# An mLSTM, gMLP and channel-mix kernel: the block mask's load moved forward, and two small copies given to GpSimd

## The chip, the cores and the metric

The kernel runs on one NeuronCore of a Trainium2 chip. The metric is the device time of one execution in microseconds. Engines are named as in the profile: PE is the matrix engine (PEld its weight loads), DVE the vector engine, ACT the scalar engine, POOL is GpSimd, SP is the engine that issues nearly all transfers. A q behind a name (SPq) means the engine's instruction queue.

## The reference

Three stages follow each other; the output of one is the input of the next. B is 2, H is 8 heads, S is 768 tokens, D is 40.

```python
# stage 1: a gated recurrence, token by token (m is the running maximum of the gates)
C = f_stab * C + i_stab * outer(v_t, k_t)          # per batch and head, 40 x 40
n = f_stab * n + i_stab * k_t
y_t = sigmoid(o_t) * (C @ q_t) / max(|n . q_t|, 1)
# stage 2, on x = y as (B, S, 320)
h = relu(x @ w_in); u, v = h[:512], h[512:]
x = (u * (w_spatial @ layernorm(v) + b_spatial)) @ w_out
# stage 3: channel mix with the token before
xk, xr = mu * x + (1 - mu) * x_prev                 # two sets of mu
out = sigmoid(xr @ w_r) * (relu(xk @ w_k) ** 2 @ w_v)
```

The output is float32, and so are the inputs, except `w_in`, `w_out`, `w_k`, `w_v` and `w_r`, which come in float64.

## The kernel before, in words

**Tiling.** The recurrence is computed in chunks of 128 tokens: 6 chunks for each of 2 batches, taken alternately, which makes 12 positions. At a position PE forms scores of queries and keys (`sc`, line 463), the logarithms of the decays (`ld`, lines 471 to 497), their product with the values (`av`, line 599), the chunk's contribution to the state (`sp`, line 533) and the state's contribution to the tokens (`ip`, line 570). ACT takes the exponential of `ld` into `dt` (lines 479 and 505), DVE multiplies `dt` by the scores (lines 489 and 508), and `normalise` (from line 602) makes the chunk's output `x`. PE transposes `x` through `tp` (line 646); ACT and DVE split the transposed tile into two float32r parts, `xg` (lines 660 and 235). Stage 2's first product (`up`, `vp`) is then drawn between the positions. Stages 2 and 3 follow as long rows of float32r products with three terms each (line 671).

**The mask.** A product of eight heads in groups of three puts blocks that belong to different heads side by side. The block mask, three columns of 120 rows, cuts them out. It is loaded into `bm_raw` with a stride of 41 elements (so each element stands alone in memory), copied by ACT to `bm_sb` (line 546), and used by ACT at the first chunk of each batch (`cn`, line 548) and by DVE later (line 552).

**The 64 repeated columns.** `x` has 384 columns, of which 320 come from the recurrence. The last 64 repeat columns 256 to 319 so that the third transpose fills both halves of its 128 rows. The copy (lines 627 and 628) is done by ACT at the first two positions and by POOL at the other ten.

**Weights.** A float64 weight is loaded as raw words and turned into a high and a low float32r part: ACT makes `wsq` (line 274), DVE or ACT the bits (`wbits`), DVE combines them (lines 284 and 288), ACT writes the high part (line 297), POOL the low part (line 235). For `w_u` there are three slices, split one after the other in the first 33 us; `wsq` has two buffers.

**What sets the order.** While the program is built, a planner keeps a clock of its own and an estimate for each step. Every chain of steps, such as `("P", 0.2, ...)`, names its engine (V is DVE, A is ACT, P is POOL) and a cost; the planner always issues the step that it expects to start first, and PE's tasks with it. The result is a fixed list for PE, ACT, DVE and POOL, which each work through in that order. Where the planner expects PE to wait, it inserts short matmuls with unused results (`wp`, line 363). SP issues transfers in the order of the calls, and a transfer waits until the eighth before it has landed.

**Lines to follow.** The loads at the start stand at lines 370 to 372: the two gates, the identity, four tiles of output gates (`og`), then the first queries and keys (`qk`). The next group, with `bm_raw` sixth among its eight, stands at lines 874 to 876. The gate tiles of the chunks from the third on are computed on DVE at lines 407 to 416 (`f`, `i`, in 96 rows), and PE transposes them at line 423 (`gpsc`).

Of the kernel before, what the change touches and what calls it, by code (L numbers as in the profile page):

```python
# [7 lines left out]
F32 = mybir.dt.float32  # L8
# [10 lines left out]
def tile_mlstm_gmlp_channelmix(  # L19
# [25 lines left out]
    SEQ = [6 * b + c for c in range(6) for b in range(2)]  # L45
    P = 128
    H, D = 8, 40
    DA = D + 1
# [3 lines left out]
    DM = H * D  # L52
# [6 lines left out]
    vec, act, pool, pe = nc.vector, nc.scalar, nc.gpsimd, nc.tensor  # L59
    sync = nc.sync  # L60
# [4 lines left out]
    at = tc.alloc_tile_pool(name="at", bufs=1, side="right")  # L65
# [59 lines left out]
    def use(e, cost, t=None):  # L125
        free[e] = max(free[e], clock[0] if t is None else t) + cost
        return free[e]
# [45 lines left out]
    def chain(key, *steps, ready=None):  # L173
        running.append(Chain(key, steps, clock[0] + 0.2 if ready is None else ready, 0.0))

    def finish(*keys, stall=True):
        for k in keys:
            while any(b[0] == k or b[0][0] == k for b in back):
                if not force_feed():
                    break  # L180
            for c in [c for c in running if c.has(k)]:
                while c in running and c.has(k):
                    advance(c.start(), skip=c)
                    if not c.open():
                        finish(split[0], stall=False)
                    if c in running and c.has(k):
                        issue(c)
        if stall:
            at_least(max([done.get(k, 0.0) for k in keys], default=0.0))
# [25 lines left out]
    def load(out, in_, kb, after=0.0):  # L215
        sync.dma_start(out=out, in_=in_)  # L216
        dma_free[0] = max(dma_free[0], after, clock[0] - 1.0) + max(0.5, kb / (360.0 if clock[0] > 20.0 else 230.0))
        return dma_free[0] + 1.8

    def page(name, dt=F32R, n=PG, keys=()):  # L220
        own("pg", 12, *keys)
        return base.tile([P, n if dt == I64 else PG], dt, tag="pg", name=name, bufs=12)[:, :n]
# [80 lines left out]
    def rows3(t, w):  # L303
        return t[:, :3 * w].rearrange("p (a b) -> p a b", a=3)
# [6 lines left out]
    fg = gp.tile([16, S], F32, name="fg")  # L311
    ig = gp.tile([16, S], F32, name="ig")
# [17 lines left out]
    def load_qk(i):  # L330
        b, c = divmod(i, NCH)
        t = at.tile([P, 2, 4, P], F32, tag="qk", name=f"qk{i}", bufs=2)
        for hh in range(2):
            e = load(t[64 * hh:64 * hh + D], qk[b, c, hh], 164)
        st["q", i], st["k", i] = t[:, 0], t[:, 1]
        st["at", i] = e

    def load_kv(i):
        b, c = divmod(i, NCH)
        n = H * D + H * DA + (3 * P if c > 0 else 0)  # L340
        t = at.tile([P, H * D + H * DA + 3 * P], F32, tag="kvq", name=f"kvq{i}", bufs=2)
        note(("kv", i), load(t[:, :n], kvq[b, c, :, :n], n * 0.5))
        st["kt", i] = t[:, :H * D].rearrange("p (h d) -> p h d", h=H)
        st["vt", i] = t[:, H * D:H * (D + DA)].rearrange("p (h d) -> p h d", h=H)
        if c > 0:
            st["qc", i] = t[:120, H * (D + DA):].rearrange("p (g t) -> p g t", g=3)

    def load_o(c):
        for b in range(B):
            o = st["o", b, c] = at.tile([P, DM], F32, tag="og", name=f"og{c}_{b}", bufs=9)  # L350
            st["ot"] = load(o, o_tok[b, c // 3, :, c % 3], 164)
# [15 lines left out]
    vec.memset(unit.bitcast(F32), 0.0)  # L367
    for t in first_.values():
        vec.memset(t.bitcast(F32), 0.0)
    for a in 'f i d o0 o1 q'.split():  # L370
        dict(f=lambda: sync.dma_start(out=fg, in_=f_gate), i=lambda: sync.dma_start(out=ig, in_=i_gate),
             d=lambda: sync.dma_start(out=id_sb, in_=ident), o=lambda: load_o(int(a[1])), q=lambda: load_qk(SEQ[0]))[a[0]]()

    pool.memset(ones, 1.0)
# [227 lines left out]
    def normalise(i):  # L602
        b, c = divmod(i, NCH)
        av, spare = st.pop(("av", i)), st.pop(("spare", i))
        osl = st["o", b, c].rearrange("p (h d) -> p h d", h=H)
        nn = st.pop(("nn", i)) if c > 0 else at.tile([P, H, DA], F32, tag="nn", name=f"nn{i}", bufs=2)
        dn = at.tile([P, H], F32, tag="dn", name=f"dn{i}", bufs=2)
        x = at.tile([P, 3 * P], F32, tag="x", name=f"x{i}", bufs=2)

        finish(*[("nn", i)] * (c > 0), stall=False)  # L610

        def clip():
            vec.tensor_scalar(out=spare, in0=nn[:, :, D], scalar1=1.0, scalar2=None, op0=ALU.max)
            pool.tensor_tensor(out=osl, in0=osl, in1=nn[:, :, :D], op=ALU.mult)
            return use("P", 0.82, free["V"])

        chain(("x", i),
              ("V", 0.41, lambda: vec.tensor_tensor(out=nn, in0=nn, in1=av, op=ALU.add)) if c > 0 else
              ("A", 0.4, lambda: act.copy(nn, av)),
              ("V", 0.08, clip),  # L620
              ("V", 0.15, lambda: vec.scalar_tensor_tensor(out=dn, in0=nn[:, :, D], in1=spare,
                                                           scalar=-1.0, op0=ALU.mult, op1=ALU.max), ("av", i)),
              ("V", 0.18, lambda: vec.reciprocal(out=dn, in_=dn)),
              ("V", 0.4, lambda: vec.tensor_tensor(out=x[:, :DM].rearrange("p (h d) -> p h d", h=H), in0=osl,
                                                   op=ALU.mult,
                                                   in1=dn.unsqueeze(2).to_broadcast([P, H, D]))),
              ("P", 0.2, lambda: pool.tensor_copy(x[:, DM:], x[:, 2 * P:DM])) if SEQ.index(i) >= 2 else
              ("A", 0.2, lambda: act.copy(x[:, DM:], x[:, 2 * P:DM])))
        st["x", i] = x

    xg = {}
# [139 lines left out]
    def w_in_load(nm, j, *qs):  # L771
        W.setdefault((nm, "raw"), [])
        for q in qs:
            raw = page(f"w_in{nm}{q}", I64, PG // 2, [f"w_{nm}{x}" for x in range(3)])[:, :512]
            W[nm, "raw"].append((q, raw, load(raw, w_in[j, q], 512)))
# [84 lines left out]
    free["A"] = 8.5  # L860
    free["P"] = 3.0
    hu = [rows3(page(f"w_u{q}"), 512) for q in range(2)]
    bm_raw = at.tile([120, 3], F32, name="bm_raw")
    m2 = gp.tile([96, 2, P], F32, name="m2")
    lpk = gp.tile([96, 6 * NCH], F32, name="lpk")
    clock[0] = 5.5
# [4 lines left out]
        for w in range(2):  # L871
            st["late"] = load(m2[:, w], mg[:, w:w + S], 48, 14.0)

    for a in 'k0 v0 q6 k6 v1 b v2 n'.split():
        dict(k=lambda: load_kv(SEQ[a != "k0"]), q=lambda: load_qk(SEQ[1]), n=lambda: load_qk(SEQ[2]),
             v=lambda: w_in_load("u", 0, int(a[1])), b=lambda: load(bm_raw, blockmask[:, 0:3 * DA:DA], 2))[a[0]]()
    w_in_split("u", hu)
# [42 lines left out]
    def position(p):  # L920
# [45 lines left out]
        def n1():  # L966
            intra(i, 1)
            normalise(i)
            if nn is not None:
                load_kv(nn)  # L970
            if p == 0:
                w_in_load("v", 1, 0)
                sync.dma_start(out=mu_sb, in_=mu)
            if p == 1:
                w_in_load("v", 1, 1)
                load_o(2)
                load_o(3)
            if p == 2:
                w_in_load("v", 1, 2)
                load_o(4)  # L980
            if p == 3:
                load_o(5)
            if n is not None:
                key_weights(n)
# [225 lines left out]
    for g in range(2 * B):  # L1210
# [17 lines left out]
        for j in range(3):  # L1228
            sl = slice(j * P, (j + 1) * P)
            prs = []  # L1230
            for f in range(8):
                k0, k1 = k2t[g, f][:, 0, sl], k2t[g, f][:, 1, sl]
# [126 lines left out]
```

## Time and profile before

| | us |
|---|---|
| median of 3 runs | 308.97 |
| lowest, highest | 307.27, 309.54 |
| the profiled execution's own time | 308.54 |
| its span, first to last instruction | 305.5 |

| engine | busy us | share of the span |
|---|---|---|
| PE | 294.4 | 96% |
| DVE | 218.5 | 72% |
| ACT | 172.4 | 56% |
| POOL | 140.3 | 46% |

Times in the rows count from the start of the span. A row of the timeline gives the start, the duration, the engine, the line, the operation, out<-in, the shapes and the count; a bracket at its end is the idle time of the engine just before it, and what ended that. Engines overlap neighbouring instructions a little, so a row can start some 0.1 us before the one ahead of it ends. [...]

### The profile page before, as it was taken

The numbers are of one execution on the slowest core, as the hardware profiler recorded it, in microseconds if no ns is written. First come the engines' busy times: TensorE is split into PE (matmuls) and PEld (weight loads), VectorE is DVE, ScalarE is ACT, GpSimd is POOL, SyncE is SP. The second block draws the span as 40 slices with busy tenths as digits, with TensorE's granted clock in tenths as the row PEclk, the third lists the DMA queues.
The fourth block names the chain that finished last, engine by engine and source line by source line (L and its number), as shares of the span: only waits on it lengthen the run. The fifth ranks groups of instructions, "written<-read, shape, count | busy, mean of one in ns | idle before, by whom it ended". The sixth has DMA issues, their size and how long they took to land.

```text
span 305.5 us, 6000 instructions
## 1 busy us (share of the span) xinstructions
PE 294.4 (96%) x2233; PEld 273.3 (89%) x2233; DVE 218.5 (72%) x440; ACT 172.4 (56%) x383; POOL 140.3 (46%) x167
## 2 busy tenths in 40 slices
PE   8998898999889999999999999999999999999995
PEld 6776787787778887999999999999999999999995
DVE  7768696856697787746879989898856755745611
ACT  3764587676865555653254654686936845734610
POOL 5143324526679774733556637484426305303500
PEclk9999999999999999999999999999999999999999
DMA  6959665333223411554115212221010010000001
GB/s 154 291 165 288 195 226 171 137 116 114 56 69 98 138 46 50 174 157 165 43 45 172 81 41 86 89 86 44 3 43 21 2 43 24 0 35 32 1 21 43
DMA packets 13939, 28.77 MB, mean 94 GB/s; under 512 B 2407, under 2 KB 7783, under 8 KB 13911
## 3 DMA queue, kind: packets, MB, share of 16 engines
q1 hardware_dynamic: 13879, 28.33, 29.4%
q8 instruction: 17, 0.28, 0.4%
q0 software_dynamic: 32, 0.07, 0.2%
q14 instruction: 11, 0.09, 0.1%
HBM read 26.20 MB, written 1.97 MB: 92 GB/s over the span
## 4 chain that ended last, share of the span: by engine, by line
PE 71%; DVE 9%; ACT 6%; POOL 5%; DMA 4%; issue 2%; SPq 1%; POOLq 0%; DVEq 0%; ACTq 0%
PE spp L671 16%; PE kp L671 15%; PE vv L671 14%; PE wop L671 7%; PE up L671 5%; PE rp L671 5%; DMA bm_raw<-in_blockmask_dram 3%; PE vp L671 2%; DMA qk<-in_qk_dram 2%; POOL vn L235 2%; PE sc L463 1%; DVE sb L728 1%; DVE dt L508 1%; PE av L599 1%; SPq L216 1%
## 5 line engine op out<-in xcount | busy, mean ns | idle before, releaser
L1202 POOL TENSOR_TENSOR sq<-sq 128x384 f32<-128x384 f32 x32 | 29.9, 941 | 47.9 <-ACT sq L1201 47.8
L671 PE MATMUL spp<-wsp,vn 128*128 128x384 f32 x288 | 50.4, 334 | 0.0
L671 PEld LDWEIGHTS spp<-wsp,vn 128*128 128x128 f32 x288 | 49.9, 188 | 0.0
L671 PE MATMUL kp<-xk,wk 128*128 128x384 f32 x256 | 45.3, 334 | 0.0
L671 PEld LDWEIGHTS kp<-xk,wk 128*128 128x128 f32 x256 | 44.4, 188 | 0.0
L671 PE MATMUL vv<-wv,k 128*128 128x320 f32 x288 | 42.9, 309 | 0.0
L671 PEld LDWEIGHTS vv<-wv,k 128*128 128x128 f32 x288 | 42.4, 188 | 0.0
L235 DVE TENSOR_TENSOR k<-sq,k 128x384 fp32r<-128x384 f32 x32 | 26.2, 820 | 13.6 <-ACT k L1203 13.6
L671 PE MATMUL up<-xg,w_u 128*128 128x256 f32 x192 | 31.0, 295 | 0.0
L671 PE MATMUL vp<-w_v,xg 128*128 128x512 f32 x96 | 29.0, 417 | 1.9 <-ACT vr L740 0.9
L1099 POOL TENSOR_TENSOR vs<-vs,u 128x384 f32<-128x384 f32 x16 | 19.8, 1237 | 22.5 <-DVE vs L1098 21.1
L671 PEld LDWEIGHTS up<-xg,w_u 128*128 128x128 f32 x192 | 25.8, 190 | 1.0 <-DVE xg L235 0.2
L1201 ACT ACTIVATE sq<-kp 128x384 f32<-128x384 f32 x32 | 15.6, 490 | 16.8 <-PE kp L671 14.8
L284 DVE SCALAR_TENSOR_TENSOR wbits<-wsq,wbits 128x320 int32<-128x320 int32 (+1 forms) x27 | 20.9, 774 | 4.4 <-ACT wsq L274 3.5
L671 PE MATMUL wop<-gt,wo 128*128 128x384 f32 x128 | 22.8, 334 | 0.0
L671 PEld LDWEIGHTS wop<-gt,wo 128*128 128x128 f32 x128 | 22.2, 188 | 0.0
L671 PEld LDWEIGHTS vp<-w_v,xg 128*128 128x128 f32 x96 | 17.0, 189 | 5.7 <-ACT vr L740 1.4
L1242 DVE TENSOR_TENSOR ob<-rs,vv 128x320 f32<-128x320 f32 x12 | 5.8, 487 | 20.4 <-PE vv L671 19.3
L235 POOL TENSOR_TENSOR vn<-vr,vn 128x512 fp32r<-128x512 f32 x12 | 15.4, 1287 | 6.8 <-ACT vn L750 6.8
L1100 ACT CAST gt<-vs 128x384 fp32r<-128x384 f32 x16 | 8.2, 512 | 18.0 <-POOL vs L1099 18.0
L288 DVE SCALAR_TENSOR_TENSOR wsq<-wraw,wbits 128x320 int32<-128x320 int32 (+1 forms) x21 | 17.2, 821 | 0.3
L1141 DVE SCALAR_TENSOR_TENSOR tm<-x,mu_sb,tm 128x384 f32<-128x384 f32 x24 | 17.1, 748 | 0.0
(184 smaller groups left out, 571.4 us busy)
## 6 DMA issues: line engine op xcount, KB each, us to landing
kvq<-in_kvq_dram SPq DMA_DIRECT2D x10, 516.0 KB
qk<-in_qk_dram SPq DMA_DIRECT2D x24, 160.0 KB
wraw<-in_w_k_dram SPq DMA_DIRECT2D x6, 512.0 KB
wraw<-in_w_v_dram SPq DMA_DIRECT2D x8, 320.0 KB
wraw<-in_w_sp_dram SPq DMA_DIRECT2D x12, 192.0 KB
og<-in_o_tok_dram SPq DMA_DIRECT2D x12, 160.0 KB
out_dram<-ob SPq DMA_DIRECT2D x12, 160.0 KB
w_inu<-in_w_in_dram SPq DMA_DIRECT2D x3, 512.0 KB
```

The source lines that it names most:

```text
L216: sync.dma_start(out=out, in_=in_)
L235: eng.tensor_tensor(out=out, in0=a, in1=b.bitcast(F32), op=ALU.subtract)
L284: vec.scalar_tensor_tensor(out=t["bits"], in0=t["sq"].bitcast(I32), scalar=3, in1=t["bits"], op0=ALU.logical_shift_left, op1=ALU.bitwise_or)
L288: vec.scalar_tensor_tensor(out=t["sq"].bitcast(I32), in0=t["high"], scalar=SIGN, in1=t["bits"], op0=ALU.bitwise_and, op1=ALU.bitwise_or)
L463: pe.matmul(st["sc", i, x][:, h * P:(h + 1) * P], k_[64 * x:64 * x + D, h, :], q_[64 * x:64 * x + D, h, :], start=True, stop=True)
L671: pe.matmul(out[0], l, x, start=j == 0, stop=j == len(prs) - 1)
L1099: ("P", 1.29, lambda: pool.tensor_tensor(out=vs, in0=vs, in1=ut[b][:, d, sl], op=ALU.mult)),
L1100: ("A", 0.51, lambda: act.copy(gt[:, 0], vs)), ("V", 0.7, lambda: sub(vec, gt[:, 1], vs, gt[:, 0])))
L1141: return lambda: vec.scalar_tensor_tensor(out=t[:, c], in0=x[:, c, 1:], scalar=mu_sb[:, w, c:c + 1], in1=t[:, c], op0=ALU.mult, op1=ALU.add)
L1201: chain(("k2", g, f), ("A", 0.49, lambda: act.activation(out=sq, in_=ps, func=AF.Relu), ("kp", g, f)), ("P", 0.96, lambda: pool.tensor_ten ...
L1202: ("P", 0.96, lambda: pool.tensor_tensor(out=sq, in0=sq, in1=sq, op=ALU.mult)),
L1242: vec.tensor_tensor(out=ob, in0=rs, in1=ps, op=ALU.mult)
```

## The change

The load of `bm_raw` is issued fourth, right behind the identity, and no longer between the second and the third slice of `w_u`. The copy of the 64 columns goes to POOL at all twelve positions.

```diff
-    for a in 'f i d o0 o1 q'.split():
-        dict(f=lambda: sync.dma_start(out=fg, in_=f_gate), i=lambda: sync.dma_start(out=ig, in_=i_gate),
+    bm_raw = at.tile([120, 3], F32, name="bm_raw")
+    for a in 'f i d b o0 o1 q'.split():
+        dict(b=lambda: load(bm_raw, blockmask[:, 0:3 * DA:DA], 2), f=lambda: sync.dma_start(out=fg, in_=f_gate), i=lambda: sync.dma_start(out=ig, in_=i_gate),
...
-              ("P", 0.2, lambda: pool.tensor_copy(x[:, DM:], x[:, 2 * P:DM])) if SEQ.index(i) >= 2 else
-              ("A", 0.2, lambda: act.copy(x[:, DM:], x[:, 2 * P:DM])))
+              ("P", 0.2, lambda: pool.tensor_copy(x[:, DM:], x[:, 2 * P:DM])))
...
-    bm_raw = at.tile([120, 3], F32, name="bm_raw")
...
-    for a in 'k0 v0 q6 k6 v1 b v2 n'.split():
+    for a in 'k0 v0 q6 k6 v1 v2 n'.split():
```

The planner makes another order of the second edit. On SP only `bm_raw` moves. Three places where the lists differ:

ACT at the first transpose, before: the copy of the 64 columns, then the high part of the first slice of `w_u`, then the split of the transposed `x`.

```order
L278 ACTIVATE wbits<-w_inu_162 128x512
L628 COPY x_347<-x_347 128x64
L297 CAST w_u_148<-wsq 128x512
L660 CAST xg_412<-tp_413 128x3x128
L274 ACTIVATE wsq<-w_inu_165 128x512
```

And with the change:

```order
L278 ACTIVATE wbits<-w_inu_163 128x512
L660 CAST xg_407<-tp_408 128x3x128
L297 CAST w_u_150<-wsq 128x512
L274 ACTIVATE wsq<-w_inu_165 128x512
L278 ACTIVATE wbits<-w_inu_165 128x512
```

The copy has left ACT, and the split of `x` stands ahead of the first slice of `w_u`. On PE the transposes `tp` of that `x` stand behind ten of the short matmuls that follow `av`, where they stood behind twelve; two more stand behind them.

ACT some ten instructions later, before: the second copy and the high part of the third slice of `w_u` stand ahead of the exponential of the fourth position.

```order
L414 CAST Axc<-i_77 96x128
L628 COPY x_489<-x_489 128x64
L297 CAST w_u_148<-wsq 128x512
L479 ACTIVATE dt_0_539<-ld_0_532 128x512
L426 ACTIVATE egc<-gpsc 128x192
L910 ACTIVATE dec<-dps 120x36
```

And with the change:

```order
L415 CAST Axc<-i_77 96x128
L480 ACTIVATE dt_0_538<-ld_0_531 128x512
L427 ACTIVATE egc<-gpsc 128x192
L909 ACTIVATE dec<-dps 120x36
L297 CAST w_u_150<-wsq 128x512
```

The third slice stands behind the exponential `dt` and behind `egc` and `dec`, which it preceded.

DVE around the gate tiles `f` and `i`, before:

```order
L288 SCALAR_TENSOR_TENSOR wsq<-w_inu_162,wbits 128x512
L284 SCALAR_TENSOR_TENSOR wbits<-wsq,wbits 128x512
L407 TENSOR_TENSOR f_76<-f_76,m_151 96x128
L408 TENSOR_TENSOR i_77<-i_77,m_151 96x128
L409 TENSOR_TENSOR f_76<-f_76,m_151 96x128
```

And with the change:

```order
L288 SCALAR_TENSOR_TENSOR wsq<-w_inu_163,wbits 128x512
L408 TENSOR_TENSOR f_76<-f_76,m_152 96x128
L409 TENSOR_TENSOR i_77<-i_77,m_152 96x128
L410 TENSOR_TENSOR f_76<-f_76,m_152 96x128
L411 SCALAR_TENSOR_TENSOR f_76<-ones,f_76 96x128
```

The bits of the third slice (line 284) no longer stand between the second slice and the gate tiles; they stand behind the `x` of the second position, fifteen instructions later.

## Rows read from the trace of the kernel before

**Rows 1.** The chain that ended last, 8 to 33 us: start, us, what.

```profile
8.79 8.23 DMA bm_raw<-in_blockmask_dram
```

**Rows 2.** Windows: us, busy (count) of PE, PEld, DVE, ACT, POOL; clock, DMA, GB/s.

```profile
60.00:305.50 245.50, 239.34 (x1682) 228.65 (x1678) 172.22 (x320) 135.51 (x296) 116.45 (x128) 1.00 0.21 67
```

**Rows 3.** Timeline of PE, 14 to 37 us.

```profile
14.91 1.13 PE L463 MATMUL sc<-qk 40*128 40x128 f32 x14 [0.28 <-DMA qk<-in_qk_dram]
15.97 0.83 PE L533 MATMUL sp<-kvq,kw 128*120 128x123 f32 x6
...
18.80 2.02 PE L363 MATMUL wp<-id_sb 128*128 128x256 bf16 x12
20.66 0.49 PE L646 MATMUL tp<-id_sb,x 128*128 128x128 f32 x3
...
27.38 0.48 PE L471 MATMUL ld<-unit,Axb 128*128 128x512 f32 x1 [0.59 <-DVE dt L489]
...
29.50 0.30 PE L423 MATMUL gpsc<-id_sb,i 96*128 96x96 f32 x1 [0.71 <-DVE i L416]
...
32.27 0.80 PE L533 MATMUL sp<-kvq,kw 128*120 128x123 f32 x6 [1.22 <-ACT dt L479]
...
34.06 0.49 PE L646 MATMUL tp<-id_sb,x 128*128 128x128 f32 x3
...
36.04 0.86 PE L671 MATMUL up<-xg,w_u 128*128 128x256 f32 x5
```

**Rows 4.** Timeline of ACT, 17 to 32 us.

```profile
17.04 0.19 ACT L546 COPY bm_sb<-bm_raw 120x3 f32<-120x3 f32 x1 [1.84 <-DMA bm_raw<-in_blockmask_dram]
17.32 0.82 ACT L548 ACTIVATE cn<-sp,bm_sb 40x123 f32<-40x123 f32 x3
...
20.19 0.25 ACT L628 COPY x<-x 128x64 f32<-128x64 f32 x1
20.52 0.62 ACT L297 CAST w_u<-wsq 128x512 fp32r<-128x512 f32 x1
21.19 0.48 ACT L660 CAST xg<-tp 128x384 fp32r<-128x384 f32 x1
...
24.16 0.59 ACT L479 ACTIVATE dt<-ld 128x512 f32<-128x512 f32 x1
...
31.01 0.62 ACT L297 CAST w_u<-wsq 128x512 fp32r<-128x512 f32 x1 [0.36 <-DVE wsq L288]
31.54 0.59 ACT L479 ACTIVATE dt<-ld 128x512 f32<-128x512 f32 x1
```

**Rows 5.** Timeline of SP's queue.

```profile
2.18 1.85 SPq L216 DMA_DIRECT2D og<-in_o_tok_dram  x4
...
16.85 0.59 SPq L216 DMA_DIRECT2D m<-mg  x1
```

**Rows 6.** Waits of SP's queue, 16 to 17.6 us: us, times, longest.

```profile
SPq L216 <- DMA w_inu<-in_w_in_dram: 0.6, 1, 0.6
```

**Rows 7.** Timeline of POOL, 24 to 47 us.

```profile
24.33 1.27 POOL L235 TENSOR_TENSOR w_u<-wsq,w_u 128x512 fp32r<-128x512 f32 x1 [1.85 <-ACT w_u L297]
...
46.88 0.56 POOL L627 COPY x<-x 128x64 f32<-128x64 f32 x1 [1.59 <-PE up L671]
```

**Rows 8.** Timeline of DVE, 19 to 30 us.

```profile
19.80 0.68 DVE L288 SCALAR_TENSOR_TENSOR wsq<-w_inu,wbits 128x512 int32<-128x512 int32 x1
...
23.78 0.69 DVE L284 SCALAR_TENSOR_TENSOR wbits<-wsq,wbits 128x512 int32<-128x512 int32 x1 [0.62 <-ACT wbits L278]
24.39 1.36 DVE L407 TENSOR_TENSOR f<-f,m 96x128 f32<-96x128 f32 x1
...
25.88 0.28 DVE L409 TENSOR_TENSOR f<-f,m 96x128 f32<-96x128 f32 x1
...
26.64 0.69 DVE L489 TENSOR_TENSOR dt<-dt,sc 128x512 f32<-128x512 f32 x1
...
28.82 0.63 DVE L416 TENSOR_SCALAR i<-i,f 96x128 f32<-96x128 f32 x1
```

## The prediction

> **What bounds the kernel now.** I read three views in turn. First the chain of waits that ended last. The conspicuous piece that is not compute is the mask's load: issued at 8.79 us, landed 8.23 us later, at 17.02 [rows 1]. It invites the conclusion that 8 us can be had; the next views show why not. Second, the busy time by windows: from 60 us to the end PE works 239.34 of 245.50 us at the full granted clock [rows 2]. That stretch has little to give, and since it works through one fixed list, what the head of the program gains or loses reaches the end nearly one for one. Third, PE's timeline of the head. PE has no gap at 17 us, where ACT waits for the mask: it works through its list and through the short `wp` matmuls. What it does wait for stands in the brackets [rows 3]: 0.28 us at 14.91 for the second position's `qk`, 0.59 at 27.38 for a product on DVE, 0.71 at 29.50 for the gate tile `i` of DVE, 1.22 at 32.27 for the exponential `dt` of ACT. Only these four can be shortened or lengthened by the change; together they are 2.8 us of 305.5.
>
> **The mask's wait itself.** ACT stood idle for 1.84 us before `bm_sb` [rows 4]. But the next instruction, `cn` at 17.32, also needs PE's `sp`, which ran from 15.97 to 16.80 [rows 3]. An early mask therefore gives ACT at most 17.32 - 16.80 = 0.52 us, and the next paragraph takes most of it back. I put it at nothing: `cn` stays near 17.3, and with it `x` of the first position.
>
> **The load in its new place.** Four issues of `og` take 1.85 us of SP's queue, 0.46 each [rows 5]. One more in front of them sends everything up to the second position's `qk` a slot later. PE was already waiting for that `qk` at 14.91, so PE goes on at 15.37: a loss of 0.46 that its gapless list carries on. The other price is what the small elements cost the transfer engines. SP's `m` at 16.85 waited for a `w_inu` slice to land, the transfer ahead of the mask [rows 5, 6]; the mask landed at 17.02, 0.17 behind it. So the bounds are 0.17 (only the engines' time counts) and 0.63 (both). I take the slot, 0.46, because the first transfers leave SP one slot apart, which is more than the 0.17.
>
> [...]
>
> **The first copy on POOL.** ACT's copy took 0.25 us at 20.19 [rows 4]. POOL's has been seen to take 0.56 [rows 7]; `x` is done just after DVE's `wsq` starts at 19.80 [rows 8], so the copy ends near 20.45. The transposes now stand behind ten `wp` and not twelve. Twelve took 18.80 to 20.66, 0.155 each; ten, with PE 0.46 later, put the transposes at 20.66 - 0.31 + 0.46 = 20.81. The copy is covered by the `wp`; were they gone, PE would wait some 0.3 us for it.
>
> **The first slice of `w_u` gets later.** ACT's split `xg` follows the transposes by 0.53 (21.19 against 20.66), so 21.34. The cast of `w_u`, which was ahead of it at 20.52, now follows it: 21.34 + 0.48, less an overlap of 0.1, is 21.72, a delay of 1.20 us. Behind it hang POOL's low part, the `wsq` buffer that this frees, the third slice's bits, the second slice and the exponential `dt` at 24.16 [rows 4], now 25.36 to 25.95.
>
> **DVE still comes out ahead.** Before, DVE did the bits of the third slice at 23.78, then `f` at 24.39, which took 1.36 us where the same form takes 0.28 at 25.88; the product `dt` followed at 26.64 [rows 8]. During `f` POOL ran its `w_u` part from 24.33 to 25.60 [rows 7], and `f` ended 0.15 us after it. Now the bits are out of the way. DVE's second `wsq` may be held by POOL's first part (21.72 + 0.62 + 0.08 + 1.27 = 23.7), takes 0.68, then `f`, `i`, `f` at 0.28 and a scan of 0.42 end near 25.6. The product then waits for the exponential only: 26.0, 0.64 earlier. PE's wait at 27.38 goes: PE arrives there at 26.79 + 0.46 = 27.25 and finds the bank free.
>
> [...]
>
> **The gate tile `i`.** From the product at 26.64 to the end of `i` at 28.82 + 0.63 = 29.45 DVE needed 2.81 us [rows 8]. From 26.0 that ends at 28.81. But POOL's second `w_u` part, 1.2 us later than at 24.33, now falls into these instructions. One hold as long as that of `f`, 1.36 - 0.28 = 1.08, would make it 29.89. Between the two I take the middle, 29.35. PE's second `gpsc` starts 0.05 later, at 29.40.
>
> **The wait of 1.22 us.** PE's `sp` at 32.27 would have started at 31.05 without it, 1.55 behind `gpsc`. The exponential it waited for ran at 31.54, late because the cast of the third `w_u` slice stood ahead of it at 31.01 and itself waited for DVE [rows 4]. In the new order it comes before that cast; its `ld` starts at 27.25 and it can run before 29. So `sp` starts at 29.40 + 1.55 = 30.95, not 32.27: **a gain of 1.32 us**. With `i` at 28.81 or 29.89 it is 1.86 or 0.78; with the load's bounds the ends are 2.15 and 0.61.
>
> **What is late next.** The third slice: bits and combination follow `x` of the second position (29.35 + 0.4 + 0.5 = 30.3), 0.69 and 0.68, so 31.6; cast 32.2; POOL's part of 1.27 until 33.5. Its first reader is the run of `up` at 36.04 [rows 3], 34.7 by then: 1.2 us to spare. The second copy on POOL follows `x` at 30.3; if both DVE steps hold it off, it is done by 31.9, and its transposes, at 34.06 before, come at 32.74. Both are covered; without cover each would cost what it is late. Nothing further on changes its order.
>
> **The sum.** 308.54 - 1.3 = 307.2 for the execution that was profiled, whose span is 305.5 and which has 3.0 us around it. The median of the runs is 0.43 higher; from it the sum gives 307.7. I predict between them, **307.4**.
>
> **Rivals.**
> [...]
> - *More goes than I count.* If the earlier load costs only 0.17 and DVE is not held at all, the gain is 2.15; if waits further on, which I leave unchanged, shrink as well (PE is idle 6.2 us after 60 us), 3 to 4. This gives 304.9 to 306.5. For it: POOL and DVE meet at other moments throughout. Against: most of that list is unchanged.
> - *Slower: the mask holds up the first loads.* The transfer took 8.23 us, and how much of it was its own 360 elements is not separable in these rows beyond the 0.17 above. If at the head they delay `qk` by a third of that, 2.7 us, the time is 308.97 - 1.3 - 0.46 + 2.7 = 309.9. It decides from a delay of 0.46 + 1.32 = 1.8 us. Against: the slot and the 0.17.
> - *The load's move does nothing* is part of the forecast: `sp` covers its wait.
>
> **Chances.** Forecast 0.56 (306.5 to 308.1), waits back 0.19, more 0.19, slower 0.06. The range leaves out the far half of "more" and the slower case: 305.6 to 309.2. A measurement of this kernel can tell 1%, 3.1 us, from no change. Below 305.9 lies half of "more" and a sliver of the forecast: 0.13. Above 312.0 lies half of the slower case: 0.04 with what I have not thought of. The rest, 0.83, is within 1%.
>
> **What would show it.** `bm_sb` runs near 15.3 without a wait; PE's `sc` waits some 0.5 us longer for `qk`; `f` on DVE starts before 24.4 and takes less than 1.36; PE's `sp` (the one at 32.27) waits for nothing and starts near 31; the transposes at 34.06 come near 32.7. A wait at `sp` or `gpsc` as long as before, or `sc` later than 16.0, would make the prediction wrong, as would a shift at 36 us that has gone or doubled by the end.

## The result, and the profile after

| | before | changed |
|---|---|---|
| median, us | 308.85 (20 runs) | 305.31 (20 runs) |
| lowest, highest | 306.63, 312.05 | 304.53, 312.68 |
| ratio, 95% interval | | 0.9895 [0.9873, 0.9918] |

The change gains 3.5 us, about 1%. The ratio is taken over fast executions, within 1.5% of the fastest of their kernel (19 and 17 of the 20). 307.4 was predicted, and 305.6 to 309.2 as the range: the waits that the prediction named do go, but the change is worth more than they are long. The first profiled execution of the changed kernel was interrupted by one late transfer (further down), so the rows of after come from its repetition, whose span is 303.2 us and whose mean granted clock is 0.998.

PE's timeline of that execution, to be held against [rows 3]: start, duration, engine, line, operation, out<-in, shapes, count, and in brackets the idle time just before it and what ended that.

```profile
9.46 0.39 PE L476 MATMUL ld<-mask 128*128 128x512 bf16 x1 [1.68 <-ACT mask L859]
...
15.09 1.24 PE L464 MATMUL sc<-qk 40*128 40x128 f32 x16
...
27.02 0.48 PE L472 MATMUL ld<-unit,Axb 128*128 128x512 f32 x1
...
28.59 0.30 PE L424 MATMUL gpsc<-id_sb,i 96*128 96x96 f32 x1 [0.15 <-DVE i L417]
...
29.98 0.73 PE L534 MATMUL sp<-kvq,kw 128*120 128x123 f32 x6
...
31.70 0.49 PE L646 MATMUL tp<-id_sb,x 128*128 128x128 f32 x3
...
33.67 0.86 PE L671 MATMUL up<-xg,w_u 128*128 128x256 f32 x5
```

The waits of 0.59 us at `ld` and 1.22 us at `sp` are gone, and 0.15 of the 0.71 us at `gpsc` is left. `sp` starts 2.29 us earlier (29.98 against 32.27), the transposes 2.36, `up` 2.37, and the span is 2.3 shorter than the 305.5 of before: what the head gains reaches the end whole. A wait that the first trace did not have stands at 9.46; it is explained with the load, below.

ACT's timeline, to be held against [rows 4]:

```profile
16.05 0.18 ACT L547 COPY bm_sb<-bm_raw 120x3 f32<-120x3 f32 x1
17.21 0.82 ACT L549 ACTIVATE cn<-sp,bm_sb 40x123 f32<-40x123 f32 x3 [0.98 <-PE sp L534]
...
21.16 0.48 ACT L660 CAST xg<-tp 128x384 fp32r<-128x384 f32 x1 [0.66 <-PE tp L646]
21.54 0.62 ACT L297 CAST w_u<-wsq 128x512 fp32r<-128x512 f32 x1
...
28.17 0.60 ACT L480 ACTIVATE dt<-ld 128x512 f32<-128x512 f32 x1 [1.04 <-PE ld L476]
...
30.82 0.62 ACT L297 CAST w_u<-wsq 128x512 fp32r<-128x512 f32 x1 [1.37 <-DVE wsq L288]
```

The mask is there before ACT wants it, and `cn` then waits for PE's `sp`, at 17.21 against 17.32. The exponential `dt` runs at 28.17, not 31.54, and the third slice's cast waits for DVE behind it, where it delays nobody.

DVE, against [rows 8], and then POOL, against [rows 7]:

```profile
22.43 1.62 DVE L288 SCALAR_TENSOR_TENSOR wsq<-w_inu,wbits 128x512 int32<-128x512 int32 x1
23.98 0.28 DVE L408 TENSOR_TENSOR f<-f,m 96x128 f32<-96x128 f32 x1
...
25.82 0.69 DVE L490 TENSOR_TENSOR dt<-dt,sc 128x512 f32<-128x512 f32 x1 [0.71 <-ACT dt L480]
26.43 0.37 DVE L413 TENSOR_TENSOR i<-i,f 96x128 f32<-96x128 f32 x1
...
27.91 0.63 DVE L417 TENSOR_SCALAR i<-i,f 96x128 f32<-96x128 f32 x1
```

```profile
19.83 0.63 POOL L628 COPY x<-x 128x64 f32<-128x64 f32 x1 [0.59 <-DVE x L625]
22.24 1.27 POOL L235 TENSOR_TENSOR w_u<-wsq,w_u 128x512 fp32r<-128x512 f32 x1 [1.77 <-ACT w_u L297]
25.37 1.28 POOL L235 TENSOR_TENSOR w_u<-wsq,w_u 128x512 fp32r<-128x512 f32 x1 [1.87 <-ACT w_u L297]
```

POOL's first part of `w_u` now lies beside DVE's `wsq`, which takes 1.62 us where it took 0.68 [rows 8], and DVE has the time for it. The second part, 25.37 to 26.65, lies beside the product `dt`, which takes its usual 0.69; the step of `i` that starts in its last 0.2 us takes 0.37, 0.09 more than the 0.28 of the other steps of this form.

### The profile page after: what moved, and what is told of

The parts are those of the page before. It is cut to its first block, busy times and chain, and to the rows that moved or that the text cites. A ratio compares the mean times of both kernels' runs of the same rounds, so it can differ in the third digit from the quotient of the medians.

```text
span 307.9 us, 5999 instructions
## 1 busy us (share of the span) xinstructions
PE 296.8 (96%) x2233; PEld 275.9 (90%) x2233; DVE 218.6 (71%) x440; ACT 172.5 (56%) x381; POOL 141.1 (46%) x169
## 4 chain that ended last, share of the span: by engine, by line
PE 77%; ACT 6%; DVE 6%; POOL 4%; DMA 2%; issue 2%; SPq 1%; POOLq 0%; ACTq 0%; DVEq 0%
PE spp L671 16%; PE kp L671 14%; PE vv L671 14%; PE wop L671 7%; PE up L671 6%; PE rp L671 5%; PE sc L464 3%; PE vp L671 2%; PE av L600 2%; PE sp L534 2%; POOL vn L235 2%; DMA og<-in_o_tok_dram 1%; DVE sb L728 1%; PE wp L363 1%; PE ip L571 1%
## 5 line engine op out<-in xcount | busy, mean ns | idle before, releaser
L671 PE MATMUL up<-xg,w_u 128*128 128x256 f32 x192 | 32.1, 304 | 0.0
L671 PEld LDWEIGHTS up<-xg,w_u 128*128 128x128 f32 x192 | 26.9, 198 | 0.9
```

The source lines that it names most:

```text
L671: pe.matmul(out[0], l, x, start=j == 0, stop=j == len(prs) - 1)
```

## The experiments

Theory 1: the gain is the new order that the copies' edit makes. Theory 2, its rival: the mask's load, whose 8 us lie on the chain [rows 1]. Where several kernels are compared they ran on one chip beside the kernel before. "Mean clock" is TensorE's granted clock over an execution's span, in parts of full speed.

**The two edits apart, and both kernels again.** Before each other: 308.99 us (23 runs, 306.82 to 312.37).

> The kernel before once more, with the span of each run beside its time. Every theory: 308.9 us, ratio 1.000. It tells how much of a run's time lies outside the span: 3.0 us in the profiled execution of the kernel before, 1.8 in most runs of the changed one. If that difference belongs to the kernels, about 1 us of the gain was never in the span; if the kernel before also shows 1.8 us in most runs, the whole gain is in the span.

309.2 us (12 runs), ratio 1.0011 [0.9982, 1.0041]. In the median 1.8 us of an execution lie outside its span, as in the changed kernel: the whole gain is in the span, and the 3.0 us around the span of the profile before belong to that one execution.

```diff
-    for a in 'f i d o0 o1 q'.split():
+    for a in 'f i d b o0 o1 q'.split():      # mask's load only; copies as before
...
```

> Only the mask's load is moved; the order on all compute engines is that of before. Theory 1 (the gain is the order that the copies' edit brings): 308.6 to 309.2 us, since the mask's wait on ACT vanishes but PE's waits of 0.6, 0.7 and 1.2 us at its ld, gpsc and sp stay. Theory 2 (the mask's early landing is the gain): 306 to 306.5 us. In both, PE's wait for the second position's qk tells the price of the load's new place: 0.46 us more by the forecast, none by the trace of the changed kernel.

308.95 us (12 runs), ratio 0.9997 [0.9964, 1.0031]. PE, ACT, DVE and POOL have the order of before. At full clock (a mean clock of 0.995 or more) the median span is 305.9 us (6 executions), against 306.1 (7) for the kernel before beside it.

```diff
-              ("P", 0.2, lambda: pool.tensor_copy(x[:, DM:], x[:, 2 * P:DM])) if SEQ.index(i) >= 2 else
-              ("A", 0.2, lambda: act.copy(x[:, DM:], x[:, 2 * P:DM])))
+              ("P", 0.2, lambda: pool.tensor_copy(x[:, DM:], x[:, 2 * P:DM])))   # copies only
```

> Only the copies go to GpSimd, with the order that follows from it; the mask's load stays where it was. Theory 1: 305.5 to 306.5 us, sp near 30 us with no wait before it. Theory 2: 308 to 308.9 us, ACT still waits 1.8 us for the mask and PE's waits stay. If both edits are needed together, neither this nor the mask alone passes half of the gain of 3.3 us.

304.95 us (6 runs), ratio 0.9883 [0.9847, 0.9919]: 0.55 under the values expected. In its profile `sp` starts at 29.87 without a wait.

> The changed kernel once more, for a profile at the full granted clock throughout. Every theory: 305.3 us, ratio 0.989. In the profile that came with the result PE waited 2.3 us at about 50 us for the rows rl to land and the granted clock was 0.86 from 35 to 60 us; if that stall is a chance of that execution, this one has no such wait and a span near 303.0; if it belongs to the kernel, the wait is here too.

305.19 us (6 runs), ratio 0.9889 [0.9856, 0.9923]. The whole gain is the copies' edit: theory 1 stands, theory 2 falls. ACT's rows above show why the mask is worth nothing: the wait of 0.98 us for PE's `sp` takes the place of its own.

**Order or engine.** The copies' edit does two things: another engine copies, and the planner makes another list of it. Beside these two the kernel before took 308.54 us (24 runs, 306.18 to 313.14).

```diff
-              ("P", 0.2, lambda: pool.tensor_copy(...)))
+              ("P", 0.2, lambda: pool.tensor_copy(...) if SEQ.index(i) >= 2 else act.copy(...)))      # new order, ACT copies
```

> The changed kernel's order of instructions, with the mask's load at its early place, but the first two copies of the 64 columns are done by ACT, at the places in ACT's list that follow from that order (ahead of the split xg, and ahead of the exponential dt of the fourth position). Theory 1 (the order is the gain, not the engine that copies): nearly all of the gain stays. The second copy waits for x of DVE, near 29.3 us, and the exponential behind it for the copy, so PE's sp that stood at 32.27 us before and stands at 29.98 with the change comes at 30.1 to 30.5; time 305.3 to 305.9 us. Rival (ACT gains because it no longer copies): most of the gain goes, 307.5 to 309 us.

305.75 us (8 runs), ratio 0.9912 [0.9874, 0.9950]. ACT's timeline, then PE's:

```profile
29.85 0.24 ACT L629 COPY x<-x 128x64 f32<-128x64 f32 x1 [2.37 <-DVE x L625]
30.00 0.59 ACT L480 ACTIVATE dt<-ld 128x512 f32<-128x512 f32 x1
```

```profile
30.73 0.80 PE L534 MATMUL sp<-kvq,kw 128*120 128x123 f32 x6 [0.24 <-ACT dt L480]
```

The copy now stands in front of the exponential and holds it until `x` is there, so 0.24 of PE's wait of 1.22 us stays. `sp` is 0.2 later than the latest value expected; the time is as expected. Most of the gain stays, but not all: at full clock the median span is 303.95 us (8 executions), against 303.4 (6) for the changed kernel's repetition and 305.3 (9) for the kernel before beside it.

```diff
-              ("P", 0.2, lambda: pool.tensor_copy(...)))
+              ("P" if SEQ.index(i) >= 2 else "A", 0.2, lambda: pool.tensor_copy(...)))                # POOL copies, old order
```

> POOL does all twelve copies and the mask is loaded early, but the planner still reckons the first two copies as ACT's, so that every other instruction of PE, ACT, DVE and POOL stands where it stood before. Theory 1 (order): PE's wait of 1.2 us at sp stays, because the third slice's cast still stands ahead of the exponential; 308.3 to 309.2 us. Rival (the engine): two copies of 0.25 us fewer on ACT bring most of the gain, 305 to 306.5 us.

308.43 us (12 runs), ratio 0.9995 [0.9964, 1.0025]. ACT, then PE:

```profile
30.68 0.62 ACT L297 CAST w_u<-wsq 128x512 fp32r<-128x512 f32 x1 [3.06 <-DVE wsq L288]
31.20 0.59 ACT L480 ACTIVATE dt<-ld 128x512 f32<-128x512 f32 x1
```

```profile
31.93 0.80 PE L534 MATMUL sp<-kvq,kw 128*120 128x123 f32 x6 [1.22 <-ACT dt L480]
```

ACT has two copies less to do and idles 3.06 us in their place; the wait of 1.22 us stands as in [rows 3]. At full clock the median span is 305.3 us (6 executions), and so it is in the kernel before. So the order is most of the gain. The engine that copies is worth nothing in the old order; in the new one, where the second copy would stand ahead of the exponential, POOL's copying is worth 0.24 us of PE's wait, and by the spans some half a microsecond, which executions that overlap do not settle.

**Why 3.5 and not 2.3.** The shift in the traces is 2.3 us, the medians differ by 3.5. The executions tell where the rest is. Of 70 of the kernel before whose clock was listed beside these experiments, 47 had a mean clock under 0.995; of 32 of the changed kernel, 5.

| mean clock | before: us, span | changed: us, span |
|---|---|---|
| 0.995 and more | 307.41, 305.6 (23) | 305.14, 303.2 (27) |
| under 0.995 | 309.27, 307.4 (47) | 310.75, 309.0 (5) |
| all | 309.00, 307.0 (70) | 305.31, 303.4 (32) |

(Medians, over all rounds; number of executions in brackets.) At full clock the difference is 2.27 us; over all of them it is 3.69. The repetition of the kernel before shows one such execution. Its windows (us, then busy time and count of PE, PEld, DVE, ACT, POOL, then the granted clock, DMA share, GB/s), and PE's timeline:

```profile
28.00:32.00 4.00, 2.17 (x16) 1.47 (x15) 2.68 (x10) 1.41 (x4) 1.66 (x3) 0.93 0.99 324
32.00:38.00 6.00, 5.91 (x38) 4.83 (x39) 2.75 (x8) 1.85 (x7) 1.48 (x2) 0.50 0.24 76
```

```profile
29.33 0.30 PE L423 MATMUL gpsc<-id_sb,i 96*128 96x96 f32 x1 [0.70 <-DVE i L416]
...
32.09 1.42 PE L533 MATMUL sp<-kvq,kw 128*120 128x123 f32 x6 [1.22 <-ACT dt L479]
```

After the waits PE goes on at a granted clock of 0.50 from 32 to 38 us: `sp` takes 1.42 us where it took 0.80 in [rows 3], with the same waits ahead of it. In the profile that the prediction rests on the clock stayed at 1.00 there:

```profile
28.00:32.00 4.00, 2.34 (x18) 1.63 (x17) 2.84 (x9) 1.23 (x3) 1.66 (x3) 1.00 1.02 327
32.00:38.00 6.00, 5.73 (x69) 5.11 (x69) 4.47 (x13) 2.62 (x9) 2.42 (x3) 1.00 0.53 149
```

In the changed kernel's rows of these windows the waits of 0.59 and 1.22 us are gone, and the clock stays:

```profile
28.00:32.00 4.00, 3.85 (x45) 3.23 (x43) 3.73 (x10) 2.29 (x7) 1.56 (x3) 1.00 1.02 339
32.00:38.00 6.00, 6.00 (x65) 5.34 (x64) 5.28 (x15) 3.41 (x9) 2.60 (x4) 1.00 0.60 208
```

That the waits bring the fall was tested by filling them (`heat` inserts the short matmuls; its 23rd call stands ahead of the first `gpsc`, its 24th ahead of `sp`):

```diff
+    calls, EXTRA = [0], {23: 4, 24: 7}
...
+            calls[0] += 1
+            for _ in range(EXTRA.get(calls[0], 0)):
+                pe.matmul(wp[:, :256], junk[:, :P], junk, start=True, stop=True)
             for _ in range(n):
```

> The kernel before, with eleven more short matmuls wp on PE, whose results are unused: four ahead of the first gpsc (in the place of the wait of 0.71 us) and seven ahead of the sp that waits 1.22 us. Nothing else moves. They lie inside PE's waits, so by the waits alone nothing changes. Theory 3 (part of the measured difference is that TensorE's granted clock falls to half in some executions of the kernel before, right behind its waits at 27 to 32 us, as in the profile of its repetition): the clock stays at full speed in more executions, the spans gather at 305.3 to 306.3 us, and the median is 307.2 to 307.9 us. Rival (the fall of the clock has nothing to do with these waits): 308.7 to 309.5 us, with as many executions at a mean clock under 0.995 as before.

307.0 us (12 runs), where the kernel before took 308.54; the ratio is 0.9973 [0.9946, 1.0000], whose interval just reaches no change. The median is 0.2 under the values expected. One of the 12 executions had a mean clock under 0.995, against 15 of 24 of the kernel before beside it. The median span of those at full clock is 305.2, against 305.3: at full clock the filling is worth nothing. PE's timeline, and its window:

```profile
30.96 0.93 PE L366 MATMUL wp<-id_sb 128*128 128x256 bf16 x7
31.73 0.38 PE L368 MATMUL wp<-id_sb 128*128 128x256 bf16 x2
32.56 0.80 PE L538 MATMUL sp<-kvq,kw 128*120 128x123 f32 x6 [0.45 <-ACT dt L484]
```

```profile
28.00:32.00 4.00, 3.72 (x31) 3.00 (x29) 3.13 (x10) 1.18 (x5) 1.54 (x2) 1.00 1.01 323
32.00:38.00 6.00, 5.55 (x68) 4.95 (x67) 4.18 (x12) 2.75 (x8) 2.43 (x3) 1.00 0.48 121
```

`sp` is no earlier, ACT's exponential no faster; PE merely computes while it waits. That most of the falls in the kernel before depend on these waits is shown by the counts. That all of the remaining 1.4 us is theirs is the difference of the table, not a run of its own.

The waits do not bring the fall each time, and it also came behind another wait of PE. In the profile of the mask's move alone, mean clock 0.987, PE waited 1.82 us up to 9.56 and the clock fell behind that, to 0.56 from 10 to 16 us; the later waits are there as well (0.29, 0.71 and 1.22 us), and the clock stayed at 1.00. PE's timeline, then two windows:

```profile
9.56 0.39 PE L476 MATMUL ld<-mask 128*128 128x512 bf16 x1 [1.82 <-ACT mask L860]
...
35.39 0.80 PE L534 MATMUL sp<-kvq,kw 128*120 128x123 f32 x6 [1.22 <-ACT dt L480]
```

```profile
10.00:16.00 6.00, 6.00 (x35) 4.93 (x34) 2.42 (x5) 2.19 (x5) 1.22 (x3) 0.56 1.00 309
34.00:40.00 6.00, 4.78 (x61) 4.12 (x60) 3.69 (x11) 3.44 (x9) 1.95 (x2) 1.00 0.38 130
```

**What the load's new place costs.** In the changed kernel's trace `og` is issued at 2.71, half a microsecond later than in [rows 5]:

```profile
2.18 0.49 SPq L216 DMA_DIRECT2D bm_raw<-in_blockmask_dram  x1
2.71 1.82 SPq L216 DMA_DIRECT2D og<-in_o_tok_dram  x4
```

ACT's four sigmoids wait for `og`, and the bf16 identity (`mask`, line 859) stands behind them: this is PE's wait of 1.68 us at 9.46. ACT in the changed kernel, then PE in the copies' edit alone:

```profile
8.75 0.47 ACT L355 ACTIVATE og<-og 128x320 f32<-128x320 f32 x1 [1.90 <-DMA og<-in_o_tok_dram]
9.13 0.28 ACT L859 CAST mask<-id_sb 128x128 bf16<-128x128 f32 x1
```

```profile
8.82 0.39 PE L475 MATMUL ld<-mask 128*128 128x512 bf16 x1 [0.18 <-ACT mask L858]
```

This start differs from execution to execution. Where ACT makes the tile behind all four sigmoids, it is 8.52 to 9.14 in four profiles with the load at its old place and 9.00 to 9.56 in six with the load early. If ACT makes that tile ahead of the second pair of sigmoids, the wait can be taken away:

```diff
-    open_gate(1)
     act.copy(mask[:, 1], id_sb)
+    open_gate(1)
```

> The copies' edit alone (the mask's load stays at its old place), and ACT makes the bf16 identity for the additive mask (mask, the CAST of 128x128) ahead of the second pair of output-gate sigmoids and not behind it. PE's ld that waited 0.18 to 1.8 us for it near 9 us no longer waits. Theory: where that wait was long the time falls, where it was short the exponentials behind ACT's table load take its place; 304.4 to 305.0 us, a median 0 to 0.5 us under that of the copies' edit alone. Rival: the second position's qk or ACT's exponentials take the whole wait over, 305.0 us, no change.

304.26 us (6 runs), ratio 0.9871 [0.9836, 0.9907], beside the 308.54 of before, a little under the values expected; every mean clock was 0.997 or more. It is 0.69 under the copies' edit alone, which was measured in another round; their intervals overlap, so the step's worth is not settled. Then three on one chip, beside 309.22 us for the kernel before (11 runs):

> The changed kernel, with ACT's CAST of mask ahead of the second pair of output-gate sigmoids. PE's ld no longer waits for ACT near 9 us, so nothing hides what the mask's early load takes from the first transfers. If the load costs a slot of SP's queue on the second position's qk (0.46 us in the prediction), the time is 0.3 to 0.5 us above that of the copies' edit with the same step; if it costs nothing, the two agree within 0.2 us, at about 304.3 us. In both cases under the changed kernel.

305.54 us (6 runs), ratio 0.9886 [0.9837, 0.9936]. Two of the six had a mean clock of 0.977.

> The copies' edit with ACT's CAST of mask first, the mask's load at its old place, again and on the same chip as the two others: 304.0 to 304.6 us, every execution at a mean clock of at least 0.995.

304.88 us (6 runs), ratio 0.9869 [0.9824, 0.9913]: above the value expected, but with every mean clock at 0.998 or more.

> The changed kernel beside the two others: 304.9 to 305.4 us, so 0.6 to 1.0 us above the copies' edit with the CAST first, if that step's gain is real.

305.43 us (6 runs), ratio 0.9889 [0.9843, 0.9935]. It is 0.55 above the copies' edit with the cast first, a little less than expected, and 0.11 under the changed kernel with the cast first, where the reverse was expected. PE in the changed kernel with the cast first, and in the copies' edit with the cast first:

```profile
9.92 0.49 PE L464 MATMUL sc<-qk 40*128 40x128 f32 x2 [0.16 <-DMA qk<-in_qk_dram]
11.11 1.16 PE L464 MATMUL sc<-qk 40*128 40x128 f32 x14 [0.71 <-DMA qk<-in_qk_dram]
15.86 1.13 PE L464 MATMUL sc<-qk 40*128 40x128 f32 x14 [0.23 <-DMA qk<-in_qk_dram]
```

```profile
10.29 1.16 PE L463 MATMUL sc<-qk 40*128 40x128 f32 x14 [0.35 <-DMA qk<-in_qk_dram]
15.17 1.13 PE L463 MATMUL sc<-qk 40*128 40x128 f32 x14 [0.37 <-DMA qk<-in_qk_dram]
```

With ACT's wait away PE meets the queries and keys, and with the early mask it meets them later in these two profiles: 15.86 against 15.17. At full clock the median spans are 303.5 (4 executions, 303.1 to 303.9) and 303.15 (6, 302.1 to 303.4), 0.35 apart, within the expected step of 0.3 to 0.5. The changed kernel and the copies' edit alone are 0.4 apart (303.4 and 303.0, six each); in the old order no cost shows (305.9 against 306.1 with the mask's move alone). So in the new order the early load probably costs some 0.4 us, which executions that overlap do not settle, and it brings nothing.

The lowest medians measured are those of the copies' edit with the cast first and the mask's load left where it was: 304.26 and 304.88 us. On the same chip the changed kernel is 0.55 higher, but one of its six executions lost clock; at full clock its median span is 303.2 (5 executions), against 303.15. The difference of these two kernels is not settled.

## Why the prediction was wrong, step by step

**The step that failed first is the price of PE's waits.** "Only these four can be shortened or lengthened by the change; together they are 2.8 us of 305.5" prices a wait at its own length. That holds in an execution whose clock stays at 1.00, as it did over the profile's whole span (mean 1.000). But 47 of 70 executions had a mean clock under 0.995, and their median span is 307.4 us, where it is 305.6 at full clock. With the waits filled, one of 12 had. The waits at 27 to 32 us therefore cost 2.3 us, and in many executions close to two more. At full clock the prediction's way of counting was 0.97 short (2.27 against 1.3); over all executions it was 2.4 short (3.69).

The sum also set waits of one kind of execution against times of both kinds: "308.54 - 1.3 = 307.2". The profiled execution's time lay near the median of all only by chance, since 3.0 us of it lie outside the span, where 1.8 are usual; its span of 305.5 is one of full clock. From 307.41, the median time at full clock, the same sum gives 306.1, and 305.14 was measured. And the four waits were not the only ones: in the changed kernel a fifth, up to 1.68 us at 9.46, came in.

**The second is the gate tile `i`,** which was given half a hold: "Between the two I take the middle, 29.35". It ended at 27.91 + 0.63 = 28.54. Of the 0.81 us, 0.54 is the hold that did not come, 0.18 the product, which started at 25.82 and not at 26.0, and 0.09 is DVE's other steps. The half hold was an estimate of mine from the one hold of `f` (1.36 us against 0.28). POOL's second `w_u` part met the product `dt`, and the product was not held: 0.69 us beside POOL, 0.69 in [rows 8]. `wsq` took 1.62 beside POOL's first part, 0.68 in [rows 8]. Why the one was held and the other not, no run shows. From `gpsc` to `sp` it is 1.39 us, not 1.55. With the 0.81 this makes the 0.97 us by which `sp` is earlier than predicted (29.98 against 30.95).

**The load's slot, 0.46 us,** is about the size of what the new order shows (0.35 and 0.4 at full clock, not settled), but it had not the right place. I saw it at the second position's `qk` only. In the changed kernel it mostly falls on ACT's sigmoids and so on PE's `ld` at 9.46. PE, held up there, reaches `sc` when `qk` has landed, so the two waits are one: 15.09 without a wait, against 14.91 after 0.28 us [rows 3].

What the 360 elements take of the transfer engines' time, the changed kernel's trace shows. From 3.2 to 3.8 us, behind the issue of `bm_raw`, it has packets, bytes and rate, then the share of the 16 engines' time:

```profile
DMA packets 390, 0.01 MB, mean 19 GB/s; under 512 B 381, under 2 KB 390, under 8 KB 390
q1 hardware_dynamic: 390, 0.01, 47.4%
```

That is 0.28 us of all sixteen engines for the mask's elements and some thirty other packets (in the same stretch the kernel before has 7 packets under 512 B), more than the 0.17 that the prediction took as its lower bound, but spread over 0.6 us. As SP's slot is about as long (0.53, from 2.18 to 2.71), no run separates the elements from the slot.

**Right were:** the mask's wait, worth nothing (0.9997 alone); the first copy, 0.63 us where 0.56 was taken, covered by the `wp`; the first slice of `w_u` at 21.54 (21.72 predicted), and the `wsq` behind it, held as foreseen; `f` back to 0.28; the exponential ahead of the third cast; the two covers at the end, since no wait came in at the second copy's transposes or at `up`.

**The rivals.** "More goes than I count" was the case in its time (304.9 to 306.5), but not in its cause: DVE was indeed hardly held, while the load probably did cost about its slot, and the rest was the clock and not waits further on. That the waits come back, 0.19 of the chances, no run shows: `sp` starts at 29.98 without one. "The mask holds up the first loads" is refuted by the run of the mask alone (0.9997).

**What stays open.** Five of 32 executions of the changed kernel still lose clock, and two of six when it has the cast first; none of eight did with the copies on ACT, and none of 18 in the new order with the mask's load at its old place. In one profile PE had waited 1.60 us for `mask` at 9.30, and the clock fell behind that (its window):

```profile
10.00:16.00 6.00, 6.00 (x36) 4.93 (x35) 2.82 (x5) 2.38 (x5) 1.03 (x2) 0.55 1.01 317
```

Waits of 1.68 and 1.50 us there, in the changed kernel's other profile and in the kernel with the waits filled, left the clock at 1.00. In the changed kernel's first profile, span 307.9, it was a transfer of gate rows that came late. PE's timeline, and the window behind it:

```profile
50.06 0.50 PE L496 MATMUL ld<-rl,lt 128*128 128x512 f32 x1 [2.32 <-DMA rl<-Lxc]
```

```profile
48.00:60.00 12.00, 9.94 (x81) 8.63 (x82) 6.13 (x14) 4.73 (x11) 5.54 (x7) 0.72 0.43 137
```

Whether the early load makes such executions more frequent isn't settled by these counts: in the old order six of 12 with the mask's move alone had a mean clock under 0.995, and six of 12 with POOL copying.

## What to carry to other kernels

Before a sum is made on one profile, look at the mean clock of several executions: if it varies, a wait in a busy stretch of PE can cost more than its length (here the median span is 307.4 us under a mean clock of 0.995, 305.6 from there on), and filling it with unused matmuls shows how much (here 307.0 us against 308.54, an interval that just reaches no change). A step's engine label in a planner is an edit of the whole order; take the order and the engine apart before crediting either. A small load is priced by what stands behind it on its queue, followed to the engine that needs that first.

## What the runs showed of the hardware

- Behind the same waits of PE (0.7 and 1.2 us, one soon after the other) the granted clock fell to 0.50 from 32 to 38 us in one profile of the kernel before and stayed at 1.00 in another: executions of one kernel differ.
- Eleven matmuls of no use, laid into such waits, made a kernel's median 1.5 us shorter (307.0 against 308.54, an interval that just reaches no change), and the executions with a mean clock under 0.995 fewer (1 of 12 against 15 of 24).
- 360 elements of 4 bytes, loaded with a stride, took at most 0.28 us of the sixteen transfer engines' time, spread over about 0.6 us.
